# Second layer of a two-layer network: seven fp32 products replaced by three single passes over 12-bit parts

## The chip, the core and the metric

The kernel runs on one core of one Trainium2 chip. The metric is the device time of one execution in microseconds; shown for a kernel is the median of its runs. The profile is of one execution, whose own time is given beside its span. TensorE (PE) multiplies matrices, and each matmul has a weight load (PEld) of its own; VectorE (DVE) and ScalarE (ACT) do elementwise work, each in the order in which it was given; SyncE (SP) issues the DMAs, and waits in its own order too. Matmul results lie in eight banks of PSUM[...]; everything else lies in SBUF or in DRAM.

## What is computed

A gated linear attention with a recurrent state, and a network with a squared ReLU on its output:

```python
B, H, S, D = 4, 8, 768, 48
for t in range(S):
    state = alpha[:, :, t, :, None] * state + np.einsum('bhd,bhe->bhde', k[:, :, t], v[:, :, t])
    y[:, :, t] = np.einsum('bhd,bhde->bhe', q[:, :, t], state)
x = np.ascontiguousarray(y.transpose(0, 2, 1, 3)).reshape(B * S, H * D)   # 3072 x 384
h = np.maximum(x @ w_in, 0.0)                                           # w_in 384 x 2048
out = (h * h @ w_out).astype(np.float32)                                # w_out 2048 x 384
```

All inputs but the weights are fp32. The weights arrive as fp64 and are turned into fp32 by the kernel.

## The kernel before

The 3,072 tokens are 24 blocks of 128, block n being chunk n // 4 of batch n % 4. Four blocks are a group; there are six groups, g = 0 to 5 in the code (the change's "two to six" are g = 1 to 5). In group 0 the kernel loads and converts the weights and runs both layers plainly. From g = 1 on, a group is two stages of TensorE work, written out by hand, and the attention of the blocks of the next group is woven between their instructions.

**First layer, `layer_in`.** It follows the text `LAYER` word by word. `P` is a product (two matmuls of 128x256) into one of eight banks `b0` to `b7`: four from the pool `ps_att`, four from `ps_ffn`. A word such as `u3=u5+b7` is a DVE addition of 128x512, `u3=b1` a copy on ACT, `R` a ReLU and `Q` a square on ACT, `V` both at once on DVE. It is a scheme with fewer products than the plain one, over sums of parts of `x` (`sum_x`, 11 DVE operations, due at the end of the group before) and of `w_in`. Its results are the squared hidden values: `u0` to `u7` and `v0` to `v7`, 16 tiles of 256 hidden values by 256 tokens. `S` words add two of them for the second layer. `between` runs other steps ahead of a given word.

**Second layer, `ffn_product`.** A seven-product scheme for a two by two split matrix. For each product and each of four parts r there are four fp32 matmuls of 128x192, each of which shows as two records. 28 parts make a group. Between them DVE updates the operands (`s`, `a21`), and when a product ends, DVE and ACT add its result (`us`, `osb`); `store` writes the output. In g = 1, `sum_w_out` makes the sums of weight parts, 16 DVE operations of 384 columns.

**Weaving.** `weave(units, events)` issues the units in order; each has a cost, and an event is issued ahead of the first unit at which the running cost has reached its time. `attention(pairs, scale)` makes the events of a pair of blocks: by `PLAN`, `ln` (ACT) and `sp` (DVE splits the logarithm into two fp32r parts) come first, at 2.5 `cs` (TensorE sums the logarithms, `eb` and `ei` take exponentials on ACT), at 3.5 to 5 `mk` and `mq` (DVE scales keys and queries), at 6.5 `turn` (transposes), at 7 `kc` and `qc` (ACT copies), at 9.5 and 10.5 `ga` and `gb`: scores, state sums and the products `y` of the pair before, with DVE's masks and state updates. `gb` ends with `ev`, twelve ACT copies of the pair's `y` into `x`. `sum_x` follows at 11.5. The code issues in that order, and every engine keeps it. The pairs of a group before the change are

```python
pairs = [(0, n, True), (11.5, n + 2, True)]
if g == 1:
    pairs = [(0, n - 2, False), (6.8, n, True), (13.4, n + 2, True)]
```

The lines that matter: L674 products of the first layer, L616 all DVE additions made by `combine`, L685 `V`, L691 and L694 `Q` and `R`, L780 products of the second layer, L742 the plain second layer of group 0, L267 and L268 `cs` in fp32r, L283 `mk` and `mq`, L532 `turn`, L555 `ev`.

Of the kernel before, what the change touches and what calls it, by code (L numbers as in the profile page):

```python
# [25 lines left out]
def kernel(  # L26
# [64 lines left out]
    w_out = [consts.tile([128, NJ // NW, DM], FP32, name=f"w_out{i}") for i in range(NW)]  # L91
    HM, NR2 = DM // 2, NJ // 4
    tsum = [kept(f"t{i}_", NR2, [128, 2, HM]) for i in (1, 2, 4)]

    def flat(t):
        return t.rearrange("a x y -> a (x y)")

    lent = {("a", 2): flat(tsum[0][0]), ("a", 3): flat(tsum[0][1])}  # L100
    for x, n, i in (("q", 2, 6), ("q", 3, 7), ("k", 3, 5)):
        t = lent[x, n] = flat(w_out[i])[:, 0 : 64 * H].rearrange("a (h d) -> a h d", h=H)
        nc.gpsimd.memset(t[:, :, D:64], 0.0)
# [18 lines left out]
    def load_weights(i):  # L122
        dst = (w_in + w_out)[i]
        dt = moe_w_in.dtype
        raw = dst if dt == FP32 else raw_pool.tile(list(dst.shape), dt, tag="raw", name="raw")
        raws[i] = raw
        if i < NW:
            src = moe_w_in[:, i * DF // NW : (i + 1) * DF // NW]
            nc.sync.dma_start(out=raw, in_=src.rearrange("(k r) f -> r k f", r=128))
        else:  # L130
            i -= NW
            src = moe_w_out[i * DF // NW : (i + 1) * DF // NW, :]
            nc.sync.dma_start(out=raw, in_=src.rearrange("(j r) m -> r j m", r=128))
# [5 lines left out]

    def convert_first(i):  # L140
        if moe_w_in.dtype == FP32:
            return
        w = (w_in + w_out)[i].rearrange("a k f -> a (k f)")
        n = w.shape[1]
        words = raws.pop(i).rearrange("a k f -> a (k f)").bitcast(U32)
        words = words.rearrange("a (n h) -> a n h", h=2)
        lo, hi = words[:, :, 0], words[:, :, 1]
        power = cv_pool.tile([128, n], U32, tag="power", name="power")
        upper = cv_pool.tile([128, n], U32, tag="upper", name="upper")
        nc.vector.tensor_scalar(  # L150
            out=power, in0=hi, scalar1=20, scalar2=0x7FF,
            op0=ALU.logical_shift_right, op1=ALU.bitwise_and,
        )
        nc.vector.tensor_scalar(
            out=upper, in0=hi, scalar1=0xFFFFF, scalar2=None, op0=ALU.bitwise_and
        )
        half[i] = w, lo, hi, power, upper
# [72 lines left out]
    hid = [consts.tile([128, 2, GB * C], FP32, name=f"hid{i}") for i in range(NJ // 2)]  # L230
# [331 lines left out]
    def st(n):  # L562
# [34 lines left out]

# [7 lines left out]
        Pv4+w1x15 Qu2 v7=v5+b6 Pv3+w0x0 Ru7=-u7 u1=b4-u1 Pu7+w18x1 Qu7 v6=u1-b5 Pv1+w7x2 Su1  # L605
        Ru1=+b7 Pv4+w10x14 v0=v4-b3 Qu1 Pv6+w9x16 Rv4=+b1 V+v0 Pv5+w4x2 Qv4 v7=v7+b4 Pu2+w12x0
        v6=v6+b6 Rv7=-v7 v2=v2+b5 Pv0=w19x3 Qv7 V+v6 Rv2=+v2 Pv0+w6x1 Sv1 Qv2 Pu2+w7x2 v5=v5+b0
        Pu7=w19x3 Ru4=+b2 V+v5 Pu7+w6x1 Qu4 Pv4+w18x1 u5=u5+b7 V+u5 Rv1=+b4 Qv1 Su0 Sv0
    """
    FIRST = "u"  # L610

    acc, ws, sums = {}, {}, {}
# [10 lines left out]
    def w_slot(i):  # L623
# [4 lines left out]
        if r not in ws:  # L628
            ws[r] = raw_pool.tile([128, 3, 2, 256], FP32, tag="raw", name="ws")
            if r == 2:  # L630
                sums.update({3: ws[r][:, 2]})
# [12 lines left out]
    def sum_x(g):  # L644
        if not xs_ready:
            a = raw_pool.tile([128, 3, 2, HT], FP32, tag="raw", name="s012")
            sums.update({r: a[:, r] for r in range(3)})
            xs_ready.append(True)
# [3 lines left out]
    xs_ready = []  # L652

    def part(name):
        c, h = divmod(int(name[1]), 2)
        return hid[2 * c + "uv".index(name[0])][:, :, h * HT : (h + 1) * HT]

    def layer_in(g, between):
# [5 lines left out]
        for n, word in enumerate(LAYER.split()):  # L664
            if n in between:
                between[n]()
# [13 lines left out]
            elif word[0] == "S":  # L680
                r = 2 * int(word[2]) + "uv".index(word[1])
                combine(((sums[r], halves(r)[1], ALU.add, halves(NR2 + r)[1]),))
# [22 lines left out]
    def sum_w_out(i):  # L705
        i, r = divmod(i, NR2)
        t1, t2, t4 = (t[r] for t in tsum)
        b11, b12 = w_out[r][:, :, 0:HM], w_out[r][:, :, HM:DM]
        b21, b22 = w_out[NR2 + r][:, :, 0:HM], w_out[NR2 + r][:, :, HM:DM]
        o, x, z = ((t1, b12, b11), (t2, b22, t1), (b12, b22, b12), (t4, b21, t2))[i]  # L710
        combine(((o, x, ALU.subtract, z),))

    def halves(j):
        return hid[j][:, :, 0:HT], hid[j][:, :, HT : 2 * HT]

    turn_r = [0]

    def ffn_in(g, j, cols=slice(0, GB * C)):
# [11 lines left out]
        nc.scalar.activation(out=hid[j // 2][:, j % 2, cols], in_=r, func=AF.Square)  # L730
# [6 lines left out]
    def ffn_out(g, t, i):  # L737
# [3 lines left out]
        for j in range(per):  # L741
            nc.tensor.matmul(  # L742
                out=acc[t][:, 0:DM],
                lhsT=hid[i][:, j, t * C : (t + 1) * C],
# [13 lines left out]
    PRODUCTS = (("1", 0), ("5", 3), ("6", 1), ("7", 2), ("2", 0), ("4", 2), ("3", 3))  # L758

    R = [0, 2, 1, 3] if FIRST == "u" else [1, 3, 0, 2]  # L760
    PARTS = [(i, r) for rs in (R[:2], R[2:]) for i in range(2) for r in rs]
    PARTS += [(i, r) for i in range(2, len(PRODUCTS)) for r in R]

    def ffn_product(g, i, r):
        name, k = PRODUCTS[i]
        first = name in "1675"
        if r == R[0] and first:
            acc[k] = ps_ffn.tile([128, 2, HM], FP32, tag="f", name="o")
        (a11, a21), (a12, a22) = halves(r), halves(NR2 + r)
        s = sums[r]  # L770
        t1, t2, t4 = (t[r] for t in tsum)
        b11, t3 = w_out[r][:, :, 0:HM], w_out[r][:, :, HM:DM]
        b21, b22 = w_out[NR2 + r][:, :, 0:HM], w_out[NR2 + r][:, :, HM:DM]
        lhs, rhs = {
            "1": (a11, b11), "2": (a12, b21), "3": (s, b22), "4": (a22, t4),
            "5": (s, t1), "6": (s, t2), "7": (a21, t3),
        }[name]
        for j in range(2):
            for t in range(2):
                nc.tensor.matmul(  # L780
                    out=acc[k][:, t, :], lhsT=lhs[:, j, t * C : (t + 1) * C], rhs=rhs[:, j, :],
                    start=(first and r == R[0] and j + t == 0), stop=(r == R[-1] and j == 1),
                    skip_group_check=True,
                )
        if name == "5":
            combine(((s, s, ALU.subtract, a11),))
        elif name == "6":
            combine(((a21, a11, ALU.subtract, a21),))
        elif name == "7":
            combine(((s, a12, ALU.subtract, s),))  # L790
        if r != R[-1]:
            return
        if name == "1":
            for h in range(2):
                acc["out", h] = cv_pool.tile([128, 2, DM], FP32, tag="upper", name="osb")
            us = cv_pool.tile([128, 2, 2, HM], FP32, tag="power", name="us")
            acc["u1"], acc["u2"] = us[:, 0], us[:, 1]
            nc.scalar.activation(out=acc["u1"], in_=acc[k], func=AF.Copy)
        elif name == "5":
            pass  # L800
        elif name in "67":
            u, new = ("u1", "u2") if name == "6" else ("u2", "u3")
            if new == "u3":
                acc[new] = acc["out", 1][:, :, HM:DM]
            nc.vector.tensor_tensor(out=acc[new], in0=acc[k], in1=acc[u], op=ALU.add)
            if new == "u3":
                nc.vector.tensor_tensor(
                    out=acc[new], in0=acc[3], in1=acc[new], op=ALU.add
                )
        else:  # L810
            h, m, u = {"2": (0, 0, None), "4": (1, 0, "u2"), "3": (0, 1, "u2")}[name]
            o = acc["out", h][:, :, m * HM : (m + 1) * HM]
            if u:
                nc.vector.tensor_tensor(out=o, in0=acc[k], in1=acc[u], op=ALU.add)
            else:
                nc.scalar.activation(out=o, in_=acc[k], func=AF.Copy)
            if name in "43":
                for t in range(2):
                    store(g, 2 * h + t, acc["out", h][:, t, :])
            if name == "3":  # L820
                acc.clear()
# [96 lines left out]
    NG, NU = NBLK // GB, len(PRODUCTS) * NR2  # L918
# [9 lines left out]
    weave(units, sorted(events, key=lambda x: x[0]))  # L928
    for g in range(1, NG):

        between = {}
        if g == 1:
            between = {3 + 10 * i: lambda i=i: sum_w_out(i) for i in range(2 * NR2)}
        layer_in(g, between)
        events = []
        if g + 1 < NG:
            n = GB * (g + 1) + 2
            pairs = [(0, n, True), (11.5, n + 2, True)]
            if g == 1:
                pairs = [(0, n - 2, False), (6.8, n, True), (13.4, n + 2, True)]  # L940
            events = attention(pairs, 1) + [(pairs[-1][0] + 11.5, sum_x, (g + 1,))]
        if g == 1:
            late = [(0.5 + i, sum_w_out, (2 * NR2 + i,)) for i in range(2 * NR2)]
            events = sorted(events + late, key=lambda x: x[0])
        weave([(1, ffn_product, (g, *u)) for u in PARTS], events)
# [30 lines left out]
```

## Time and profile before

| | us |
|---|---|
| median of 3 runs (548.89 to 550.3) | 548.97 |
| the profiled execution | 549.13 |
| its span | 547.4 |
| first layer of a group, g = 1 to 5, TensorE | 34.53 |
| second layer of g = 5, with nothing woven in | 36.41 |
| from one first layer to the next, g = 2 to 3 | 84.87 |

The groups that cost DVE and ACT most, and the matmuls of the second layer (line, engine, operation, tiles written and read, shapes, count; busy us and mean ns of one; idle time just before them and what ended it):

```profile
L616 DVE TENSOR_TENSOR hid<-hid,h 128x512 f32<-128x512 f32 x130 | 88.4, 687 | 40.5 <-PE h L674 37.0
L780 PE MATMUL o<-w_out,hid 128*128 128x192 f32 x480 | 82.3, 327 | 0.0
L780 PEld LDWEIGHTS o<-w_out,hid 128*128 128x128 f32 x480 | 78.5, 190 | 0.6
...
L691 ACT ACTIVATE hid<-hid 128x512 f32<-128x512 f32 x55 | 34.7, 631 | 1.8
```

A matmul's 327 ns run from its issue to the end of its pipeline; the distance from start to start is what it takes of TensorE. DVE has long idle times ended by TensorE, and TensorE has none.

### The profile page before, as it was taken

What the parts mean: (1) busy time and instruction counts of PE and PEld (TensorE: products, weight loads), DVE (VectorE), ACT (ScalarE), POOL (GpSimd) and SP (SyncE); (2) the same over time, 40 slices, a digit from 0 to 9 for tenths busy, and PEclk for the clock granted to TensorE, in tenths of its full rate; (3) what the DMA queues carried; (4) which work ended last, traced back from release to release, by engine and by line L of the source; (5) the groups of instructions that cost most, each with busy time, mean ns of one, the idle gap of its engine ahead of it and who ended that gap; (6) DMA issues with size and microseconds to landing.
All of it is one profiled execution on the core that took longest, in us unless ns stands there. A gap on an engine that the chain in (4) does not pass through costs nothing.

```text
span 547.4 us, 12320 instructions
## 1 busy us (share of the span) xinstructions
PE 534.2 (98%) x5226; PEld 455.3 (83%) x5226; DVE 368.6 (67%) x656; ACT 235.8 (43%) x503; POOL 5.9 (1%) x26
## 2 busy tenths in 40 slices
PE   8889999999999999999999999999999999999996
PEld 5654456656889999989999988999988999988996
DVE  4888889993898873778583677673578651577530
ACT  4568874435264354246343236542326440336100
POOL 2010000000000000000000000000000000000000
PEclk9999999999999999999999999999999999999999
DMA  9979577201001664200343300252300000100001
GB/s 162 239 191 278 148 225 204 59 16 57 1 1 30 118 112 88 66 1 0 60 90 63 85 0 1 46 94 55 88 1 0 2 2 2 57 1 0 1 1 57
DMA packets 117085, 37.02 MB, mean 68 GB/s; under 512 B 108820, under 2 KB 111912, under 8 KB 117032
## 3 DMA queue, kind: packets, MB, share of 16 engines
q1 hardware_dynamic: 117032, 36.25, 29.5%
q8 instruction: 41, 0.67, 0.5%
q14 instruction: 12, 0.10, 0.1%
HBM read 31.49 MB, written 4.75 MB: 66 GB/s over the span
## 4 chain that ended last, share of the span: by engine, by line
PE 81%; DVE 10%; ACT 4%; issue 2%; DMA 2%; SPq 0%; POOL 0%; DVEq 0%; POOLq 0%
PE o L780 33%; PE h L674 32%; PE o L742 4%; PE y L397 4%; PE sckv L421 2%; PE T L532 2%; PE sckv L447 2%; ACT power L163 1%; DMA raw<-in_moe_w_in_dram 1%; DVE w_out L176 1%; DMA raw<-in_moe_w_out_dram 1%; DVE power L172 1%; DVE power L150 1%; DVE w_in L176 1%; DVE w_out L179 1%
## 5 line engine op out<-in xcount | busy, mean ns | idle before, releaser
L616 DVE TENSOR_TENSOR hid<-hid,h 128x512 f32<-128x512 f32 x130 | 88.4, 687 | 40.5 <-PE h L674 37.0
L780 PE MATMUL o<-w_out,hid 128*128 128x192 f32 x480 | 82.3, 327 | 0.0
L780 PEld LDWEIGHTS o<-w_out,hid 128*128 128x128 f32 x480 | 78.5, 190 | 0.6
L674 PE MATMUL h<-xs,w_in 128*128 128x256 f32 x320 | 74.8, 379 | 0.0
L555 ACT COPY x<-y 32x256 f32<-32x256 f32 (+2 forms) x132 | 46.3, 365 | 59.7 <-PE y L397 56.1
L674 PEld LDWEIGHTS h<-xs,w_in 128*128 128x128 f32 x320 | 60.7, 190 | 8.3
L674 PE MATMUL h<-x,ws 128*128 128x256 f32 x200 | 49.7, 379 | 0.0
L723 PE MATMUL h<-x,w_in 128*128 128x512 f32 (+1 forms) x108 | 43.5, 550 | 3.3 <-ACT x L555 1.8
L431 DVE COPY_PREDICATED am<-halves_mask,sckv 128x256 f32<-128x256 uint32 x40 | 15.5, 441 | 43.7 <-PE sckv L447 43.7
L698 ACT COPY hid<-h 128x512 f32<-128x512 f32 x20 | 11.7, 586 | 76.7 <-PE h L674 76.7
L780 PE MATMUL o<-t,s 128*128 128x192 f32 x240 | 43.2, 328 | 0.0
L742 PE MATMUL o<-w_out,hid 128*128 128x384 f32 x128 | 42.8, 490 | 0.0
L674 PEld LDWEIGHTS h<-x,ws 128*128 128x128 f32 x200 | 38.0, 190 | 5.2
L674 PE MATMUL h<-x,w_in 128*128 128x256 f32 x160 | 40.2, 379 | 0.0
L780 PEld LDWEIGHTS o<-t,s 128*128 128x128 f32 x240 | 39.5, 190 | 0.3
L723 PEld LDWEIGHTS h<-x,w_in 128*128 128x128 f32 x108 | 20.0, 190 | 23.4 <-issue 16.3
L742 PEld LDWEIGHTS o<-w_out,hid 128*128 128x128 f32 x128 | 23.9, 190 | 16.2 <-issue 0.5
L691 ACT ACTIVATE hid<-hid 128x512 f32<-128x512 f32 x55 | 34.7, 631 | 1.8
L674 PEld LDWEIGHTS h<-x,w_in 128*128 128x128 f32 x160 | 30.4, 190 | 4.1
L674 PE MATMUL h<-xs,ws 128*128 128x256 f32 x120 | 30.0, 379 | 0.0
L694 ACT ACTIVATE hid<-hid 128x512 f32<-128x512 f32 x35 | 22.0, 628 | 16.9 <-DVE hid L616 16.6
L780 PE MATMUL o<-t,hid 128*128 128x192 f32 x160 | 28.8, 331 | 0.0
(128 smaller groups left out, 764.8 us busy)
## 6 DMA issues: line engine op xcount, KB each, us to landing
raw<-in_moe_w_in_dram SPq DMA_DIRECT2D x8, 768.0 KB
raw<-in_moe_w_out_dram SPq DMA_DIRECT2D x8, 768.0 KB
v_in<-in_v_dram SPq DMA_DIRECT2D x24, 192.0 KB
out_dram<-osb SPq DMA_DIRECT2D x24, 192.0 KB
k_in<-in_k_dram SPq DMA_DIRECT2D x23, 192.0 KB
a_in<-in_alpha_dram SPq DMA_DIRECT2D x22, 192.0 KB
q_in<-in_q_dram SPq DMA_DIRECT2D x22, 192.0 KB
last<-row SPq DMA_DIRECT2D x40, 0.8 KB
```

Of the source, the lines that this page charges most:

```text
L176: nc.vector.scalar_tensor_tensor(out=w, in0=upper, scalar=2.0**-20, in1=w, op0=ALU.mult, op1=ALU.add)
L397: ins = nc.tensor.matmul(out=ys[e][64 * half : 64 * half + D + G * e, m % 2, p // 2, t], lhsT=lhsT, rhs=rhs, start=(half, e) not in seen, ...
L431: nc.vector.copy_predicated(out=am_h(n)[:, e, n % 2], data=ps[e][:, 0], mask=halves_mask.bitcast(U32).unsqueeze(1).to_broadcast([128, NP, ...
L555: copy(out=x[to : to + m, kk, t : t + 2], in_=blk[n]["y"][e][r : r + m, :, p // 2],)
L616: nc.vector.tensor_tensor(out=o, in0=x, in1=z, op=op)
L674: nc.tensor.matmul(out=banks[b][:, i, :], lhsT=w_slot(int(w))[:, "uv".index(p), i * 128 : (i + 1) * 128], rhs=x_slot(int(x)), start=(start ...
L691: nc.scalar.activation(out=t, in_=t, func=AF.Square)
L694: nc.scalar.activation(out=part(o), in_=operand(x), func=AF.Relu, scale=1.0 if sign == "+" else -1.0)
L698: nc.scalar.copy(out=part(word[0:2]), in_=operand(word[3:5]))
L723: nc.tensor.matmul(out=ps, lhsT=w[:, kk, c0 : c0 + 128], rhs=xT[g][:, kk, cols], start=(kk == 0), stop=(kk == KM - 1),)
L742: nc.tensor.matmul(out=acc[t][:, 0:DM], lhsT=hid[i][:, j, t * C : (t + 1) * C], rhs=w_out[i][:, j, :], start=(i == 0 and j == 0), stop=(i ...
L780: nc.tensor.matmul(out=acc[k][:, t, :], lhsT=lhs[:, j, t * C : (t + 1) * C], rhs=rhs[:, j, :], start=(first and r == R[0] and j + t == 0), ...
```

## The change

Each factor of the second layer is split into parts of at most 12 bits, [...]whose matmul shows as one record. A weight w is b + l with b the rounded part; a hidden value is a + l in the same way. The product is put together from three: a with b, l with l (the weights' l scaled by 2^12), and a difference of the hidden parts with a difference of the weights' parts. The first two are accumulated in one bank per block (stage one), scaled by 2^-12 into `osb` by ACT, and the third goes to the same bank (stage two) and is added to `osb` by DVE.

In g = 1 the first five pairs p of 256 hidden values in `ORDER` are done so, and the other three as plain fp32 matmuls; in g = 2 the weights of these three are split. The rounded weights stay in SBUF; `l` and `d` of the weights are written to DRAM once and read back in each later group through a ring of tiles. A unit of stage one is one pair p and one half h of the tokens: eight matmuls of 384 columns.

```diff
+    wt_pool = ctx.enter_context(tc.tile_pool(name="wt", bufs=14))
+    two_pool = ctx.enter_context(tc.tile_pool(name="two", bufs=19))
...
-        Pv4+w1x15 Qu2 v7=v5+b6 Pv3+w0x0 Ru7=-u7 u1=b4-u1 Pu7+w18x1 Qu7 v6=u1-b5 Pv1+w7x2 Su1
...
-        Pu7=w19x3 Ru4=+b2 V+v5 Pu7+w6x1 Qu4 Pv4+w18x1 u5=u5+b7 V+u5 Rv1=+b4 Qv1 Su0 Sv0
+        Pv4+w1x15 Qu2 v7=v5+b6 Pv3+w0x0 Ru7=-u7 u1=b4-u1 Pu7+w18x1 Qu7 v6=u1-b5 Pv1+w7x2 Ru1=+b7
...
+    def split_w(p):
+        b = w_out.pop(p)
+        parts_b[p] = wt("wb", FP32R)
+        nc.scalar.activation(out=parts_b[p], in_=b, func=AF.Copy, scale=NEAR)
+        parts_l[p] = wt("wl", FP32R)
+        nc.vector.tensor_tensor(
+            out=parts_l[p], in0=b, in1=parts_b[p].bitcast(FP32), op=ALU.subtract
+        )
+
+    def scale_w(p):
+        nc.scalar.activation(
+            out=parts_l[p], in_=parts_l[p].bitcast(FP32), func=AF.Copy, scale=1.0 / E
+        )
+        nc.sync.dma_start(out=dram_l[p], in_=flat(parts_l[p]))
...
+    def diff_w(p):
+        d = parts_d[p] = parts_l.pop(p)
+        nc.vector.tensor_tensor(
+            out=d, in0=parts_b[p].bitcast(FP32), in1=d.bitcast(FP32), op=ALU.subtract
+        )
+        nc.sync.dma_start(out=dram_d[p], in_=flat(d))
...
+    def split_h(n):
+        if n == 0 and not first_parts:
+            first_parts.append(raw_pool.tile([128, 3, 2, HT], FP32R, tag="raw", name="ha"))
+        a, l = first_parts[0][:, n % 3], two_k("hl", FP32R)
+        t = hid.pop(hs["units"][n])
+        nc.scalar.activation(out=a, in_=t, func=AF.Copy, scale=NEAR)
+        nc.vector.tensor_tensor(out=l, in0=t, in1=a.bitcast(FP32), op=ALU.subtract)
+        hs[n] = a, l
+
+    def diff_h(n):
+        a, l = hs[n]
+        d = hd[hs["units"][n]] = two_k("hd", FP32R)
+        nc.vector.scalar_tensor_tensor(
+            out=d, in0=a.bitcast(FP32), scalar=-E, in1=l.bitcast(FP32),
+            op0=ALU.mult, op1=ALU.add,
+        )
+
+    def of_piece(t, lhs, rhs, start=False, stop=False):
         for j in range(2):
+            nc.tensor.matmul(
+                out=acc[t][:, 0:DM], lhsT=lhs[:, j, t % 2 * C : (t % 2 + 1) * C],
+                rhs=rhs[:, j, :], start=start and j == 0, stop=stop or start,
+                skip_group_check=True,
+            )
+
+    def stage_one(g, n):
+        units = hs["units"]
+        p, h = units[n]
+        a, l = hs.pop(n)
+        for t in (2 * h, 2 * h + 1):
...
+            of_piece(t, a, parts_b[p], start=new)
+            of_piece(t, l, parts_l[p], stop=n >= len(units) - 2)
+        if n + 3 < len(units):
+            split_h(n + 3)
+            diff_h(n + 3)
...
+        if n % 2:
+            if g == 1:
+                diff_w(p)
+            else:
+                parts_l.pop(p)
...
+                to_stream and to_stream.pop(0)()
...
+    def layer_out(g):
+        order = UNITS[: len(UNITS) - 2 * len(PLAIN.get(g, ()))]
+        units = [(1, stage_one, (g, n)) for n in range(len(order))]
...
+        units += [(0.5, stage_two, (g, p, (h,))) for p, h in two_first]
+        units += [(1, stage_two, (g, p, (0, 1), p == ps[-1])) for p in ps[2:]]
+        return units
...
         if g == 1:
-            between = {3 + 10 * i: lambda i=i: sum_w_out(i) for i in range(2 * NR2)}
-        layer_in(g, between)
+            for i, p in enumerate(ORDER[:5]):
+                at(2 + 22 * i, split_w, p)
+                at(8 + 22 * i, scale_w, p)
+        else:
+            loads = ORDER[:RING]
+            if g == 2:
+                for i, p in enumerate(PLAIN[1]):
+                    at(2 + 12 * i, split_w, p)
+                    at(8 + 12 * i, scale_w, p)
+                    at(30 + 12 * i, diff_w, p)
...
+            for i, p in enumerate(loads):
+                at((70 if g == 2 else 20) + 5 * i, load_l, p)
+            for p in ORDER[RING:]:
+                to_stream.append(lambda p=p: load_l(p))
+            for p in ORDER:
+                to_stream.append(lambda p=p: load_d(p))
+        for n in range(3):
+            ready = max(done[hs["units"][n]] + 2, NWORDS - 24 + 8 * n)
+            at(ready, split_h, n)
+            at(ready + 4, diff_h, n)
         events = []
         if g + 1 < NG:
             n = GB * (g + 1) + 2
-            pairs = [(0, n, True), (11.5, n + 2, True)]
+            pairs = [(-2.5, n, True), (8.3, n + 2, True)]
             if g == 1:
-                pairs = [(0, n - 2, False), (6.8, n, True), (13.4, n + 2, True)]
+                pairs = [(-2.5, n - 2, False), (4.0, n, True), (10.5, n + 2, True)]
             events = attention(pairs, 1) + [(pairs[-1][0] + 11.5, sum_x, (g + 1,))]
...
+        for t, f, args in events:
+            if t < 0:
+                at(NWORDS - 20 + int(4 * t), f, *args)
```

`LAYER` has 101 words now. The tiles of `w_out` and of the hidden values come from the two new pools instead of constants, and tiles lent to the attention in group 0 come from the pool of hidden values.

## The prediction

> **What bounds the kernel now.** I read four views. First the page, for the shares of the engines:
>
> ```profile
> PE 534.2 (98%) x5226; PEld 455.3 (83%) x5226; DVE 368.6 (67%) x656; ACT 235.8 (43%) x503; POOL 5.9 (1%) x26
> ```
>
> Then the chain that ended last, in order of time (start, us, what). It shows whether that 98% is real, and the prices of both layers:
>
> ```profile
> 342.37 3.90 PE o L780 x24
> 346.98 5.20 PE o L780 x32
> 352.18 1.15 PE T L532 x32
> ...
> 472.28 34.53 PE h L674 x160
> 506.81 36.41 PE o L780 x224
> 543.25 0.56 DVE osb L814
> ```
>
> From 133 us on the chain is TensorE with hardly a hole. Each group is 34.53 us of first layer (160 records of 216 ns), 36.41 us of second layer (224 records of 162.5 ns) and, until g=4, some 14 us of attention for later blocks woven into the second layer. So TensorE work removed there is time won, and any wait of TensorE there is time lost. Two records stand for one fp32 matmul.
>
> Third, the timeline of TensorE around the only fp32r matmuls there are (the sums of logarithms), for the price of the new operation:
>
> ```profile
> 344.81 1.46 PE L780 MATMUL o<-t,s 128*128 128x192 f32 x8
> 345.98 0.47 PE L267 MATMUL cs<-hi,causal_r 128*128 128x384 f32 x1
> 346.29 0.34 PE L268 MATMUL cs<-lo,causal_r 128*128 128x384 f32 x1
> 346.46 0.34 PE L267 MATMUL cs<-hi,causal_r 128*128 128x384 f32 x1
> 346.64 0.34 PE L268 MATMUL cs<-lo,causal_r 128*128 128x384 f32 x1
> 346.82 0.81 PE L780 MATMUL o<-t,s 128*128 128x192 f32 x4
> ```
>
> The same tile shape as in the change (128x128 weights, 384 columns) starts every 0.17 to 0.18 us: 0.176, once, where fp32 takes two records.
>
> Fourth, the timeline of DVE and ACT, for paces and waits, and the busy time by stretch at the end of the first layer of g=2 (us, PE, PEld, DVE, ACT, POOL):
>
> ```profile
> 247.64 0.68 DVE L616 TENSOR_TENSOR s<-hid,hid 128x512 f32<-128x512 f32 x1
> 248.25 0.68 DVE L616 TENSOR_TENSOR hid<-hid,h 128x512 f32<-128x512 f32 x1
> 248.96 0.69 DVE L685 SCALAR_TENSOR_TENSOR hid<-hid 128x512 f32<-128x512 f32 x1
> ...
> 264.04 0.55 DVE L283 TENSOR_TENSOR k_in<-k_in,inv 128x384 f32<-128x384 f32 x1
> 264.51 0.55 DVE L283 TENSOR_TENSOR q_in<-q_in,b 128x384 f32<-128x384 f32 x1
> ```
>
> ```profile
> 123.79 4.35 ACT L555 COPY x<-y 32x256 f32<-32x256 f32 x12 [9.64 <-PE y L397]
> 128.18 0.43 DVE L616 TENSOR_TENSOR xs<-xs,x 128x256 f32<-128x256 f32 x1 [4.96 <-ACT x L555]
> ```
>
> ```profile
> 248.00:253.00 5.00, 5.00 (x25) 4.40 (x24) 4.50 (x8) 4.36 (x8) 0.00 (x0) 1.00 0.00 0
> 253.00:257.50 4.50, 4.50 (x23) 3.96 (x22) 2.56 (x5) 1.73 (x3) 0.00 (x0) 1.00 0.00 0
> ```
>
> A 128x512 DVE operation costs 0.60 us if it doesn't read the one before (247.64 to 248.25), 0.72 if it does (248.25 to 248.96); one of 384 columns 0.47. DVE and ACT are nearly full just before the first layer ends. Twelve copies and the sums after them are a chain of 4.4 us plus.
>
> [...]
>
> **TensorE, part by part.** In g=2 to 5 the second layer goes from 224 records x 0.1625 = 36.4 us to 3 x 64 fp32r matmuls x 0.176 = 33.8: -2.6 each, -10.4. In g=1 five of eight pairs are in parts (120 x 0.176 = 21.1) and three stay plain fp32 without the seven-product scheme (24 matmuls of 384 columns, 48 records x 0.3225 from L742 = 15.5): 36.6, +0.2. Sum -10.2. Bounds on the pace: 0.1625 (the fp32 records) gives -22.2; 0.178 (longest fp32r) -8.4.
>
> **DVE and ACT.** Removed in a group: 4 S sums and 12 updates of the operands (0.69 each, busy) and a few adds of 0.55. Added: 16 subtractions and 16 scalar_tensor_tensor, 1.32 us a unit, and 16 ACT copies of 0.6. A unit (8 matmuls) lasts 1.41 us on TensorE, so DVE keeps up, with 7% to spare and attention on top. The ring of three `ha` means that splitting unit n+3 starts only when TensorE has left unit n: 2.8 us for ACT 0.6, DVE 0.7 and three signals: about 1.1 us spare. No wait from this alone.
>
> End of the first layer, g>=2. By the order of instructions DVE now gets, from word 69, the two log splits (pace 0.39 + 0.52, twice: 1.8 us) and three unit splits (six operations, 3.6) among the ten it had; four S go. From 247.64, where Su1 stood: 1.8, then v0, V, split, v7, v6, diff, v2, split, V, diff, v5, split, V, diff, u5, V at 0.6 (0.72 behind a dependence) ends at 259.4. TensorE ends the layer at 257.1 in any case, as the banks it needs are read earlier; so DVE is 2.3 us late.
>
> Stage one from there (zero = 257.1): cs to 0.7, units 0 to 3 until 6.35, then the transposes of `turn`, formerly 1.5 units later. They need mq1, which stands on DVE behind the splits of units 3, 4, 5: split 3 starts 3.1 (its ACT copy is behind b and inv), then 0.72, 0.6, 0.47 (mk0), 0.72, 0.6, 0.47, 0.47, 0.72, 0.6: mq1 runs 8.4 to 9.0. TensorE would be at the last eight transposes at 7.2: wait 1.7 us, x3 (g=2,3,4) = 5.1. Bounds 0 to 3 each.
>
> Copies of `ev` in gb before unit 8: ACT is blocked 4.4 us from 0.75 us after gb begins; the copy of unit 11 ends at 5.8, its subtraction at 6.6; TensorE (1.85 of gb, three units) arrives at 6.1: 0.5, x3 = 1.5. Bounds 0 to 1.3 each.
>
> g=1. Five weight splits replace 16 half-size sums: at words 68 and 90 they add 2 x 0.87 on DVE and about 1 us of waiting for ACT just where it is full, so it is some 5 us late. The second half of unit 1 needs a bank that u5 must leave: 1.9 us. mq1 comes later still, behind a `diff_w`: 2.8. And the weave counts a plain unit as 1 though it takes 5.2 us, and the group has 18 units: the last ga (20) and gb (21), and sum_x (22), fall behind the last unit. The order shows scores, y, scores, then the first layer at once. Nothing covers them: twelve copies 4.4, signals 0.3, four sums 1.5, the wait from ga to gb 0.5, less 1.1 of TensorE work: 5.6 us (4.5 to 7). Before, four units, 5.2 us of TensorE, stood behind gb there. Sum for g=1: 10.3.
>
> g=2, first layer: three weight splits and three diffs, 5.2 us of DVE by word 54, where, by the timeline, u2, u3 and u5 end under 0.5 us before TensorE reuses the bank that they read: I take 1.5 (0 to 4).
>
> At nothing: DRAM traffic, 6.3 MB a group, because each part is asked for 7 us or more before its use (cover gone: see the rivals); the last loads d6 and d7 have five units, 7 us. SP blocks in program order only. At the boundaries of g=2 to 4 gb has five units behind it, 8.9 us of TensorE against 7.0 for copies and four sums. The tail (add, store) stays. Group 0 has the same instructions in the same order.
>
> **Sum.** -10.2 + 10.3 + 1.5 + 5.1 + 1.5 = +8.2. The profiled execution took 549.13 us (span 547.4 and 1.7 to 1.8 around it; the median shown is 548.97): 557.
>
> **Rivals.** (1) The fp32r stream runs at 0.1625, if the 0.176 belongs to the short bursts: -22.2; but a unit is then 1.30 us, DVE's 1.32 binds and waits grow by about 2: 549.1 - 22.2 + 20.4 = 547. Against it: eight bursts, all 174 to 178 ns, and fp32 right behind is at 162. (2) The other side: DVE isn't late at the end of the first layer, as DVE had 1.9 us and ACT 2.8 us idle in the last window shown and could take the splits there. If its lag is under 0.7 us, the waits on turn and on the bank vanish and only the g=1 boundary and ev stay: 549.1 - 10.2 + 7.1 = 546. Against it: ten operations and six more don't fit into 8.6 us. (3) Parts from DRAM come late, behind attention loads of 1,024 packets of 192 B or a store that SP waits for. Two waits of 2 us in each of g=2 to 5: 557 + 16 = 573. For it: the DMA share reaches 0.65 in one window; against: 3 KB packets and wide margins.
>
> **Numbers.** Forecast 0.60, rival 1 0.12, rival 2 0.19, rival 3 0.09. The 0.3% that a measurement can tell from no change is 1.6 us. Rival 2 and most of rival 1 are faster, with a little from the low end of the forecast: 0.27; within 0.3%: 0.08; slower 0.65. The forecast's own range is 550 to 565; with the rivals of the other sign the range is 541 to 566. Half of the DVE waits would give about 552.
>
> **What would show it.** Second layer of g=5 near 33.8 us with starts 0.176 apart (TensorE); T behind DVE q_in in g=2 to 4 by 1 to 2 us; an idle stretch of 5 us ahead of the first layer of g=2, ended by DVE xs; unit 1 of g=1 behind DVE hid. If T waits under 0.5 us, rival 2; starts of 0.163, rival 1; waits on wl or wd, rival 3.

## The result and the profile after

The changed kernel takes 570.38 us (median of 4 runs, 567.51 to 571.65) against 548.93 (4 runs, 548.59 to 550.3): a ratio of 1.0379, interval 1.0333 to 1.0424. The profiled execution took 571.2 us, its span is 569.4. The forecast was 557, so it was right that the kernel gets slower, and 13 us short of the median.

First the page of the changed kernel: busy time, share and instructions of each engine, and the granted clock of TensorE in 40 equal slices (9 is full).

```profile
PE 537.5 (94%) x5042; PEld 446.5 (78%) x5042; DVE 415.0 (73%) x719; ACT 292.0 (51%) x603; POOL 5.9 (1%) x26
...
PEclk9999999999998999799999999989999989999999
```

TensorE's share fell from 98% to 94%, and in four slices the clock isn't full. Then the chain that ended last (start, us, what):

```profile
237.13 24.52 PE h L681 x100
...
328.36 34.53 PE h L681 x160
...
372.29 5.89 PE o L827 x24
379.27 1.43 PE y L412 x88
...
531.90 32.97 PE o L827 x190
```

The last line is the second layer of g=5 with nothing woven in. Its records are those of fp32r, the type of the new parts, one for a matmul (192 in all); they start 173 to 174 ns apart, and from first record to end the stage takes 33.7 us where it took 36.6. The first layer is 34.53 as before. So the gain is there; from the start of one first layer to the next (g=5: to TensorE's end) the rest shows:

| us | g=1 | g=2 | g=3 | g=4 | g=5 |
|---|---|---|---|---|---|
| before | 90.00 | 84.88 | 84.50 | 79.94 | 71.10 |
| after | 103.54 | 91.07 | 88.05 | 80.96 | 68.00 |

Which waits are new, by the list of waits (engine and line that waited, for what: us, times, longest):

```profile
PEld T L547 <- DVE q_in L298: 8.6, 8, 1.5
PE T L547 <- DVE q_in L298: 7.4, 7, 1.4
PEld h L681 <- ACT wb L779: 5.2, 1, 5.2
PE h L681 <- DVE xs L628: 5.1, 1, 5.1
```

The lower two are one idle stretch, that ahead of g=2; there the name of ACT's `wb` is misleading, as DVE's `xs` came last. In g=3, the timelines of DVE and TensorE show the wait of the transposes and what follows it:

```profile
369.35 0.55 DVE L298 TENSOR_TENSOR k_in<-k_in,inv 128x384 f32<-128x384 f32 x1
369.82 0.68 DVE L814 TENSOR_TENSOR hl<-hid,ha 128x512 fp32r<-128x512 f32 x1
370.61 0.69 DVE L820 SCALAR_TENSOR_TENSOR hd<-ha,hl 128x512 fp32r<-128x512 f32 x1
371.22 0.55 DVE L298 TENSOR_TENSOR q_in<-q_in,b 128x384 f32<-128x384 f32 x1
```

```profile
369.96 0.46 PE L547 MATMUL T<-ident,k_in 64*128 64x64 f32 x8
371.82 0.46 PE L547 MATMUL T<-ident,q_in 64*128 64x64 f32 x8 [1.40 <-DVE q_in L298]
372.22 1.01 PE L827 MATMUL o<-wb,ha 128*128 128x384 f32 x2
373.02 0.84 PE L827 MATMUL o<-wl,hl 128*128 128x384 f32 x2
...
375.93 0.51 PE L827 MATMUL o<-wb,ha 128*128 128x384 f32 x2
```

The scaled `q` stands on DVE behind a unit's split and difference, and TensorE loses 1.67 us. DVE and ACT keep the order of the code: in this trace the 175 DVE and 130 ACT operations of the five passes through `LAYER` stand in the order of its words. Then the same pair of matmuls takes 0.84 us until 375.6, and 0.51 after it: the records show a granted clock of one half for 3.41 us from 372.2. Such stretches begin at 174.2, 198.1 (it lies across two slices and does not show in the row above), 235.6 (two in a row), 372.2 and 460.9, each behind idle time of TensorE, and lengthen TensorE's work by 1.57, 1.57, 2.31, 1.78 and 1.57 us (distances from record to record less those usual for their kind): 8.8 us. The kernel before had none until TensorE's last matmul. The other new wait is in front of the second block's sum of logarithms in the second pair; ACT and DVE in g=3:

```profile
383.52 4.35 ACT L570 COPY x<-y 32x256 f32<-32x256 f32 x12
387.90 1.67 ACT L813 ACTIVATE ha<-hid 128x512 fp32r<-128x512 f32 x3
```

```profile
388.56 0.69 DVE L814 TENSOR_TENSOR hl<-hid,ha 128x512 fp32r<-128x512 f32 x1 [1.67 <-ACT ha L813]
389.36 0.69 DVE L820 SCALAR_TENSOR_TENSOR hd<-ha,hl 128x512 fp32r<-128x512 f32 x1
389.97 0.35 DVE L270 CAST hi<-a_in 128x384 fp32r<-128x384 f32 x1
390.35 0.56 DVE L271 TENSOR_TENSOR lo<-a_in,hi 128x384 fp32r<-128x384 f32 x1
```

Unit 11's copy `ha` stands behind the twelve copies of `x`, its split waits for that copy on DVE, and `hi` and `lo` stand behind the split: TensorE loses 2.48 us at `cs` here and 2.05 in g=2, counted in the same way.

### The profile page after: what moved, and what is told of

It is laid out like the page before. It is cut to its first block, busy times and chain, and to the rows that moved or that the text cites. A ratio compares the mean times of both kernels' runs of the same rounds, so it can differ in the third digit from the quotient of the medians.

```text
span 569.4 us, 12387 instructions
## 1 busy us (share of the span) xinstructions
PE 537.5 (94%) x5042; PEld 446.5 (78%) x5042; DVE 415.0 (73%) x719; ACT 292.0 (51%) x603; POOL 5.9 (1%) x26
## 4 chain that ended last, share of the span: by engine, by line
PE 65%; DVE 20%; ACT 10%; issue 4%; DMA 1%; DVEq 0%; SPq 0%; POOL 0%; ACTq 0%; POOLq 0%
PE o L827 26%; PE h L681 26%; PE o L737 4%; PE y L412 3%; DVE hl L814 2%; DVE hd L820 2%; ACT x L570 2%; PE T L547 1%; ACT power L178 1%; DVE hid L628 1%; PE sckv L436 1%; ACT hid L698 1%; DVE q_in L298 1%; DVE w_out L191 1%; DVE k_in L298 1%
## 5 line engine op out<-in xcount | busy, mean ns | idle before, releaser
L827 PE MATMUL o<-wb,ha 128*128 128x384 f32 x296 | 80.1, 352 | 2.3 <-ACT hid L698 2.0
L827 PE MATMUL o<-wl,hl 128*128 128x384 f32 x296 | 77.9, 345 | 0.1
L681 PEld LDWEIGHTS h<-xs,w_in 128*128 128x128 f32 x320 | 62.5, 196 | 14.2 <-ACT wb L779 5.2
L813 ACT ACTIVATE ha<-hid 128x512 fp32r<-128x512 f32 x74 | 46.0, 634 | 49.3 <-PE o L827 36.8
L814 DVE TENSOR_TENSOR hl<-hid,ha 128x512 fp32r<-128x512 f32 x74 | 50.9, 688 | 20.3 <-ACT ha L813 19.4
L827 PEld LDWEIGHTS o<-wb,ha 128*128 128x128 f32 x296 | 54.9, 196 | 4.1 <-ACT hid L698 2.3
L827 PEld LDWEIGHTS o<-wl,hl 128*128 128x128 f32 x296 | 55.5, 195 | 0.5 <-DVE hl L814 0.4
L820 DVE SCALAR_TENSOR_TENSOR hd<-ha,hl 128x512 fp32r<-128x512 f32 x74 | 51.1, 690 | 4.1 <-PE o L827 0.6
L827 PE MATMUL o<-wd,hd 128*128 128x384 f32 x256 | 46.7, 337 | 0.0
L827 PEld LDWEIGHTS o<-wd,hd 128*128 128x128 f32 x256 | 44.2, 188 | 0.4
L737 PEld LDWEIGHTS o<-w_out,hid 128*128 128x128 f32 x128 | 23.9, 190 | 16.2 <-issue 0.5
```

Source lines behind the costliest of these rows:

```text
L681: nc.tensor.matmul(out=banks[b][:, i, :], lhsT=w_slot(int(w))[:, "uv".index(p), i * 128 : (i + 1) * 128], rhs=x_slot(int(x)), start=(start ...
L737: nc.tensor.matmul(out=acc[t][:, 0:DM], lhsT=hid0[per * i + j][:, t * C : (t + 1) * C], rhs=w_out[i][:, j, :], start=(i == 0 and j == 0), ...
L813: nc.scalar.activation(out=a, in_=t, func=AF.Copy, scale=NEAR)
L814: nc.vector.tensor_tensor(out=l, in0=t, in1=a.bitcast(FP32), op=ALU.subtract)
L820: nc.vector.scalar_tensor_tensor(out=d, in0=a.bitcast(FP32), scalar=-E, in1=l.bitcast(FP32), op0=ALU.mult, op1=ALU.add,)
L827: nc.tensor.matmul(out=acc[t][:, 0:DM], lhsT=lhs[:, j, t % 2 * C : (t % 2 + 1) * C], rhs=rhs[:, j, :], start=start and j == 0, stop=stop o ...
```

## The experiments

Theory A: the loss is waits that come from the places of instructions, and on top of each the clock that idle time costs. Rivals: B, the clock drops are no cost of their own; C, DVE and ACT are full, so a wait taken away comes back; D, the traffic to DRAM. All edits are of the changed kernel. A quoted text is what was expected before the run; waits and times by group are those of the run's one profiled execution, the time measured is the median of all its executions.

### Is the clock a cost of its own?

Products that nobody reads (`keep_busy`: `ident` by `causal`) in TensorE's idle time, first in four places:

```diff
             for i, x in enumerate("kq"):
+                if m in (11, 19, 23) and x == "q":
+                    keep_busy(ps[0][:, 1].rearrange("a p t -> a (p t)")[:, 0:128], 6)
...
+                    if g == 2 and n == 0:
+                        keep_busy(banks[b][:, 0, 0:128], 22)
```

> Fp32 products whose result nobody reads (ident by causal, 128 columns) stand where TensorE waits: six ahead of the last eight transposes of three turns (the second turn of g=1, the first of g=3 and of g=4), 22 ahead of the first product of g=2. The waits themselves are left as they are. Theory A (the clock follows TensorE's own idle stretches, and the halved clock is a cost of its own): no stretch of half clock at 198, 236, 372 and 461 us, one left at 174; time 570.4 - (1.57 + 2.31 + 1.78 + 1.57) = 563, and the wait for q_in or xs ends at the same distance from what stands before it. Rival B (the clock drops are an outside disturbance of the chip, or cost nothing because the waits that follow shrink by as much): 570 or more, with as many stretches of half clock as after.

Measured: 573.36, a miss for A, and as long as B had said; but two things spoil the reading. All five stretches of half clock were gone, and four others had come, at 35.2, 182.0, 284.4 and 393.6. And the 22 products could start only at 235.0, when ACT's copies of `x` had left their bank, and so held up g=2 by 3 us. Only g=4 is a clean reading: 79.45 for 80.96. The second try fills more places, and less in each:

```diff
+    FILL = {9: 5, 11: 4, 15: 5, 17: 2, 19: 5, 21: 2, 23: 5}
...
+                if x == "q" and m in FILL:
+                    keep_busy(ps[0][:, 1].rearrange("a p t -> a (p t)")[:, 0:128], FILL[m])
...
+        if n in (17, 21):
+            keep_busy(out[:, 0:128], 6)
...
+        if g == 2:
+            keep_busy(ps_ffn.tile([128, GB * C], FP32, tag="f", name="idle")[:, 0:128], 21)
```

> As the first experiment, but with products whose result nobody reads in all the longer waits, fewer than fit (0.235 us each): five, four, five, five and five ahead of the last transposes of the first turns of g=1, the second of g=1, the first of g=2, 3, 4; two in the second turns of g=2 and 3; six ahead of the second sum of logarithms of the second pair; 21 (4.9 us for a wait of 5.6) ahead of the first product of g=2, in a bank that is free early. Theory A (idle TensorE drops the clock, in windows that no instruction chooses, and the drop costs time of its own): the waits end where they ended, at most two stretches of half clock are left (at 173 and in group 0), and the time is 570.4 - 7.2 = 563 (562 to 565.5). Rival B (the clock costs nothing of its own): 570 or more.

Measured: 566.65 (566.29 to 566.84). TensorE's timeline of this run at the same turn of g=3, and its clock by slices:

```profile
367.07 0.46 PE L559 MATMUL T<-ident,k_in 64*128 64x64 f32 x8
367.46 1.38 PE L545 MATMUL T<-causal,ident 128*128 128x128 f32 x10
368.94 0.46 PE L559 MATMUL T<-ident,q_in 64*128 64x64 f32 x8
369.33 0.62 PE L841 MATMUL o<-wb,ha 128*128 128x384 f32 x2
369.79 0.51 PE L841 MATMUL o<-wl,hl 128*128 128x384 f32 x2
```

```profile
PEclk9999999999998999999999999999999999999999
```

The wait is as long as before (1.87 us from the transposes of `k` to those of `q`, for 1.86), the matmuls behind it are at 0.51 from the second pair on, and one stretch is left. TensorE does more work and the kernel is 3.7 us faster: B is refuted. It is half of the 7.2 expected. In the profile, g=2 gave 2.6 and g=4 1.6, g=1 and g=3 nothing: four products in g=1 stood where there was no wait (0.9), and TensorE, earlier now, waited more at `y`, state sums and scores (1.1 in g=1; 2.0 for 0.4 in g=3), at products that wait for no other engine (more on these under the traffic). So the 8.8 us are what the slow stretches add to the matmuls in them; how much of it the kernel would gain without them stays open.

The cleanest price needs no filling. In g=4 three kernels (the changed one and two variants below that leave g=4 alone) had a stretch of half clock behind the wait at the turn: 80.96, 80.99 and 80.97. Two other variants that leave g=4 alone had the same wait and no such stretch: 79.37 and 79.41. With the wait filled it was 79.38. Half clock costs 1.6 us there.

When does it drop? Of the changed kernel and its variants, 15 profiles have stretches of half clock after the first 20 us. In each of them all of these begin on one grid of 3.413 us; in the changed kernel's, the five places lie 7, 11, 40 and 26 steps apart. Sorted by the share of a window of this grid in which TensorE's records show it busy, all 27 windows under 52% were followed by half clock, 16 of 34 between 52 and 60%, and 7 of over 2,200 above (six of them the first window of a double stretch, itself at half clock). In the changed kernel's profile the 1.40 us of idle ahead of the transposes at 371.82 lie inside one window (368.74 to 372.15, 59% busy), and half clock follows; the 1.41 us ahead of those at 284.13 are cut in two by a boundary at 283.41 (windows 64 and 79% busy), and none follows. Windows in which the records leave 1.3 to 1.9 us idle were enough. This fits the scatter: the changed kernel's times lie 4 us apart, with a mean clock of 0.988 in the fastest execution and 0.979 in the slowest, those of the run just shown 0.6 us apart, at 0.996 to 0.999.

### Are the waits of place?

The first pair of g=2 to 4 later:

```diff
-            pairs = [(-2.5, n, True), (8.3, n + 2, True)]
+            pairs = [(-1.0, n, True), (8.3, n + 2, True)]
```

> The first pair of attention in g=2, 3 and 4 stands 1.5 units later (-1.0 for -2.5), so that the transposes have unit 4 and 5 ahead of them. Theory A: the three waits of the transposes for q_in (1.67 each) fall to under 0.3, and with them the half clock at 372 and 461 (1.78 and 1.57): 570.4 - 4.2 to 5.0 - 3.4 = 562 to 563. Rival C (DVE and ACT are simply too full in these stages, and any place gives the same wait): the wait moves to the sums of logarithms, to units 5 to 8 or to gb, and the time stays at 569 to 571.

Measured: 561.65, just under Theory A's 562 to 563. In g=2 to 4 (87.24, 85.19, 78.71) the waits for `q_in` are under 0.3, and no half clock follows the turns. But `gb` comes later too: in g=2 and 3 `cs` waited some 1.1 us for the copies of `x` to leave its bank.

The end of g=1:

```diff
+        for p in ps[2:]:
+            if p in PLAIN.get(g, ()):
+                units += [(1.85, stage_two, (g, p, (h,), p == ps[-1])) for h in range(2)]
+            else:
+                units.append((1, stage_two, (g, p, (0, 1), p == ps[-1])))
...
-                pairs = [(-2.5, n - 2, False), (4.0, n, True), (10.5, n + 2, True)]
+                pairs = [(-2.5, n - 2, False), (4.0, n, True), (9.1, n + 2, True)]
```

> In g=1 the plain units are halved and counted at 1.85 each, as they last on TensorE, and the last pair stands at 9.1, so that its gb and the sums of x have two of them and more (5 to 8 us of TensorE) behind them. Theory A: the 5.63 us of idle ahead of g=2 fall to 0 to 1, and the half clock of 235.6 to 242.4 goes with it (2.31): 570.4 - 4.6 to 5.6 - 2.3 = 562.5 to 563.5. Rival (the copies and sums wait for something else than their place): the idle stretch stays over 3 us and the time over 567.

Measured: 567.13, a miss. The idle stretch ahead of g=2 was gone, but g=1 took 103.13. The third pair's `hi` now stood on DVE ahead of the second pair's last `q_in` and itself waited 2.9 for a DMA, so that the second turn waited 4.0; and TensorE waited 1.5 for ACT's `osb`. With only `ga`, `gb` and the sums earlier (`t` is 10.25 for that pair alone):

```diff
+                    if t == 10.25 and f in ("ga", "gb"):
+                        w -= 1.2
```

> In g=1 the plain units are halved and counted at 1.85 each; the last pair keeps its place (10.25 for 10.5), only its ga, gb and the sums of x come 1.2 earlier, so that three halves (7.8 us of TensorE) stand behind gb. Theory A: nothing else in g=1 moves, the 5.63 us of idle ahead of g=2 and the half clock there go: 570.4 - 5.6 - 2.3 = 562.5 (561.5 to 565, if another idle stretch meets the window instead). Rival: as in the experiment with the whole pair moved, other waits of g=1 take most of it back: over 567.

Measured: 562.28, a hit; the idle stretch was gone and g=1 took 97.97.

The second pair's logarithms ahead of `gb`:

```diff
-                    w = t + at * scale
+                    w = t + at * scale - (0.4 if f == "sp1" and t == 8.3 else 0)
```

> In g=2 and 3 the split of the logarithms of the second block of the second pair stands on DVE ahead of gb and of unit 11, not behind them. Theory A: the waits of cs ahead of unit 9 to 11 (2.05 in g=2, 2.48 in g=3) go; unit 11 itself, whose copy stands on ACT behind the twelve copies of x, then waits 0.5 as predicted: 570.4 - 3.5 = 567 (566.5 to 568). Rival (the copies of x hold ACT long enough that unit 11 takes over the wait in full): 569.5 to 570.5.

Measured: 566.77, a hit; the waits of `cs` were gone, g=2 and 3 fell by 1.75 and 2.2. Part came back at the next turn (1.35 and 1.41 for `q_in`).

The weight splits of g=1:

```diff
-                at(2 + 22 * i, split_w, p)
-                at(8 + 22 * i, scale_w, p)
+                at(2 + 12 * i, split_w, p)
+                at(8 + 12 * i, scale_w, p)
```

> The five weight splits of g=1 stand at words 2 + 12i and 8 + 12i of the first layer for 2 + 22i and 8 + 22i, so that none is left on DVE and ACT from word 57 on. Theory A: DVE and ACT are no longer late at the end of the first layer of g=1, unit 1 waits under 0.5 instead of 2.29 + 0.56, and the half clock at 174 goes: 570.4 - 2.3 - 1.6 = 566 to 566.5. Rival C (the splits of logarithms and units alone make DVE late there, as in g=2 to 4): unit 1 still waits over 1.5 and the time is over 568.5.

Measured: 567.56, between the two. Unit 1 no longer waited 2.29 + 0.56, the half clock at 174 was gone, and g=1 fell by 3.8; but g=2 rose by 2.9 in the profiled run, though nothing was changed there: its old wait at the turn fell into a window of the clock, and half clock ran from 280.1 to 286.9.

### Does the traffic matter?

```diff
+        nc.sync.dma_start(out=spare[p], in_=dram_l[p])
...
+        nc.sync.dma_start(out=spare[NW + p], in_=dram_d[p])
```

> Behind each load of a part in g=2 to 5 stands a second transfer of the same part from DRAM to a spare place in DRAM, so that these 64 loads cause over twice the traffic. Theory A (the parts arrive long before use): no wait of TensorE for wl or wd, 570.4 within 1.5. Rival D (parts from DRAM and the queue are near their limit): waits for wl or wd of 2 us and more in each of g=2 to 5, 578 or more.

Measured: 576.59, 6.2 slower than the changed kernel. Neither theory had it right: nobody waits for `wl` or `wd`, and the traffic costs time all the same. In the profile g=2 alone lost 7.6, with three more stretches of half clock and this wait in the middle of the state sums:

```profile
322.25 0.68 PE L462 MATMUL sckv<-v_in,k_in 64*64 64x64 f32 x29
326.00 0.33 PE L462 MATMUL sckv<-v_in,k_in 64*64 64x64 f32 x3 [3.06 <-issue]
```

It lies between the 29th and the 30th of 32 like products, where no record waits for a semaphore; that is what "issue" says. What the trace has there is a DMA of 16 KB of the kind "instruction", from 323.72 on, 2.28 us before the matmul. This is no exception: of the 51 waits of over 0.4 us that the 17 profiles have inside the runs of small products (`y`, scores, state sums) from g=1 on, 50 end 2.2 to 3.0 us after such a DMA began. That TensorE waits there for its own instructions is a guess from these times; no experiment tests it. These waits add up to 1.5 us after the change and to 6.5 at twice the traffic, but also to 4.6 in the first run with products that nobody reads, so that their growth with the traffic is likely and not shown.

### Does it add up, and is there a floor?

All edits together (in g=1 also -1.5 for -2.5 and 4.5 for 4.0), then the first pair of g=2 to 4 at -2.0:

> All four edits of place together: first pair of g=2 to 4 at -1.0, last pair of g=1 with its ga, gb and sums ahead of three halves of plain units, logarithms of the second pair first, weight splits of g=1 early; and in g=1 the first pair at -1.5 for -2.5, the second at 4.5 for 4.0. Theory A (the loss of the change is waits of place and the clock that they cost, each removable alone): the gains measured one by one add up, 8.7 + 8.1 + 2.8 to 4.4, and 1 to 3 of the 3.6 for the logarithms, as part of that wait is already gone: 570.4 - 22 = 548.5 (545 to 551), level with the kernel before. Rival C (DVE and ACT are full, so a wait removed comes back elsewhere): over 554.

> As the run with all edits, with the first pair of g=2 to 4 at -2.0, between the two: its transposes stand one unit later than after the change, its gb one unit earlier than at -1.0, so that the second pair's sums of logarithms have three units, not one, between them and the copies of x that free their bank. Theory A: the wait for q_in leaves 0.3 (1.67 - 1.41), the waits of cs for ACT's copies of x (0.8 + 0.4 in g=2 and 3) go: 1 to 3 below the run at -1.0, 546.5 (544 to 550). Rival C: at or above the run at -1.0.

Measured: 554.6 and 553.77. The gains did not add up: 15.8 of the 22 us came. The profiled execution at -2.0 was the fastest of six (550.52, the others from 553.5 on). In it g=2 to 5 took 83.94, 83.21, 78.06 and 68.00: all below the kernel before, by 7.2 us in all. g=1 took 98.3, and there a removed wait had come back, as C says: unit 1 no longer waits, so the transposes came sooner and waited 1.3 and 2.6 for `mk` and `mq`, with 6.8 us of half clock. DVE there, in the run at -2.0:

```profile
177.52 0.68 DVE L814 TENSOR_TENSOR hl<-hid,ha 128x512 fp32r<-128x512 f32 x1
178.31 0.69 DVE L820 SCALAR_TENSOR_TENSOR hd<-ha,hl 128x512 fp32r<-128x512 f32 x1
178.92 0.95 DVE L793 TENSOR_TENSOR wl<-wb,wl 128x768 fp32r<-128x768 f32 x1
179.78 0.55 DVE L298 TENSOR_TENSOR q_in<-q_in,b 128x384 f32<-128x384 f32 x1
```

DVE has no gap, and a weight difference stands ahead of the last factor. So the factors of g=1 were put together, and then the differences later:

```diff
+                    if t in (-1.5, 4.5) and f[:2] in ("mk", "mq"):
+                        w = t + 3.5
...
-                diff_w(p)
+                for q in ([], [], [0], [1], [2, 3, 4])[n // 2]:
+                    diff_w(units[2 * q][0])
```

> As the run with all edits and the first pair of g=2 to 4 at -2.0; and in g=1 the four products of k and q with their factors (mk, mq) of the first and second pair stand on DVE one behind the other, at 3.5 units after the pair's start, with no unit split and no diff of weights between them. Theory A: of the turn waits left in g=1 (1.3 + 2.6 at 177 and 180, 0.85 + 1.05 at 197) under 1 is left in all, and the half clock of 179.7 to 186.5 (2.8) goes: 553.8 - 4.8 - 2 = 547 (545 to 549.5), at or under the kernel before. Rival C (DVE is full there: the unit splits pushed back by 1.9 us hold up units 5 to 7 instead): 551 or more.

> The same, and in g=1 the diffs of the weights (0.9 us each on DVE) stand two pairs of units later, behind the first turn. Theory A: where the four products together removed the waits, nothing is left to gain, 547 within 1; where some wait is left ahead of the transposes of g=1, it shrinks by up to 1.8. Rival C: the three diffs together at the end of stage one hold up the factors of the second and third pair, 1 to 3 above the run without this edit.

Measured: 549.95 with the first edit (ratio 1.0013 to the kernel before, interval 1.0003 to 1.0023), 550.45 with both; the first lies between the two theories, and the second edit gained nothing. With the first, the first turn no longer waits, but `cs` of the second pair waits 3.0 for `hi` and `lo`, and the second turn 1.8 for a `k` that arrives late. Two runs tried that place alone, without the later differences, the first with an earlier load of `k` too:

```diff
+                    if t == 4.5 and f[:2] in ("ln", "sp"):
+                        w = t - (2.0 if f[:2] == "ln" else 1.6)
...
+                            if t == -1.5:
+                                out.append((w, load, (n0 + 3, "k")))
```

> As the run with the factors together; and in g=1 the k of block 11 is asked for at the first turn, ahead of the q, not at the first ga (DVE waited 1.63 for its arrival), and the logarithms of the second pair are taken and split ahead of the split of unit 6 (cs waited 0.76 + 0.36 + 1.56 + 0.35 for them). Theory A (also the rest of g=1 is place): these 4.8 us fall to under 1.5, with the half clock at 195 (1.6): 549.95 - 4.5 = 545.5 (544 to 548), under the kernel before. Rival C (DVE and ACT have no room left in g=1, as the splits of units 6 and 7 come 1.8 us later): 549 to 551, with the wait at units 6 or 7.

> As the run with the factors together, with the logarithms of the second pair of g=1 taken and split ahead of the split of unit 6, and the load of k left where it was. Theory A: the wait of cs (3.0) goes, the wait for k of block 11 stays: 549.95 - 3 = 547. Rival C (DVE has no room there): unit 6 waits 1.5 to 2 instead, 548.5 to 550.5.

In the first, the `k` of block 11 takes the buffer of block 8's before that block's state sums, which so read the `k` of block 11: this kernel leaves out a needed `k`, and only its time is used. Measured: 551.99 and 551.24. The wait of `cs` had become one of 1.57 and 1.58 of unit 6 for its split, as C says. That isn't all: in the second the wait for the `k` of block 11, a DMA and not DVE's work, grew from 1.8 to 3.9, and half clock ran for 6.8 us in place of 3.4. Last, both places together, with the transfers of the differences off SP (in the profile of the changed kernel SP issued nothing from 173.45 to 179.06, when the first difference was done):

```diff
-        nc.sync.dma_start(out=dram_d[p], in_=flat(d))
+        nc.gpsimd.dma_start(out=dram_d[p], in_=flat(d))
```

> The same, and room is made: the diffs of the weights of g=1 stand two pairs of units later (1.9 us of DVE less ahead of the splits of units 5 to 8), and their transfers to DRAM are issued by GpSimd, so that SP does not stand ahead of the loads of k until a diff is done. Theory A (the rest of g=1 is place and queues): neither cs nor unit 6 waits over 0.5, the wait for k shrinks: 546 (544.5 to 547.5), under the kernel before. Rival C (g=1 is full for DVE): 548.5 or more.

Measured: 547.47 (546.69 to 548.16), ratio 0.9968 to the kernel before, interval 0.9956 to 0.9979: inside Theory A's range, and 0.3% faster than the kernel before (all of its seven executions lie below the eleven of that kernel beside them, 548.72 to 550.53). Its page:

```profile
PE 526.2 (96%) x5042; PEld 437.6 (80%) x5042; DVE 413.5 (76%) x719; ACT 293.5 (54%) x603; POOL 10.4 (2%) x34
...
PEclk9999999999999999999999999999999999999999
```

g=1 took 95.03, still 5.0 more than before: unit 6 waits 1.0 for its split, more than Theory A had, the second turn no longer for `k` but 1.4 for banks that DVE still reads, and a `y` product 1.9 in the way told under the traffic. DVE does nearly what it did after the change (413.5 us for 415.0); only the order is another. Which of the later differences and the freed SP counted was not tried apart.

## Why the prediction was wrong

- **The step that failed** is the sum: it counts each wait of TensorE at its own length, with TensorE's pace the same behind it. In fact idle time also halved the clock, for 3.41 us at a time: 8.8 us of slower matmuls, which no term or rival held. It is the largest part of the 14.2 between 557 and the profiled 571.2. That it costs time is shown by g=4 with and without such a stretch (1.6 us) and by filling the idle time, which gave back 3.7 in all, with the filling's own cost in it.
- TensorE: right in kind and size. Taken 0.176 us, -2.6 a group; found 0.173 to 0.174 and -3.1 (71.10 to 68.00), some 2 us more gain in all. Rival 1 (0.1625) is refuted. That all eight bursts showed 174 to 178 ns was read too widely: in the two at 281.9 and 366.8 starts lie 0.3 to 0.5 us apart.
- The turn in g=2 to 4: 1.7 each predicted, 1.67 each measured, at the instruction named. Rival 2 (DVE isn't late) falls.
- The boundary ahead of g=2: 5.6 predicted, 5.63 measured (5.30 in one stretch, 0.33 between `ga` and `gb`), mechanism as told and shown by the run that took it away. The 0.3 for signals was an estimate; in the profile 0.06 us lie between the last `y` and ACT's copies at 231.17, and 0.15 between DVE's `xs` and TensorE at 237.13.
- The rest of g=1: unit 1, 1.9 predicted, 2.29 + 0.56 measured (it ends with DVE's `u5` as told, but its first half waits already, for the bank that ACT's last `R` reads); first turn 2.8, measured 0.46 + 0.28 + 1.60; the second turn's 1.43 + 0.33 was not predicted.
- `ev`: "0.5, x3" was mis-sized. The copies hold up unit 11 as predicted, but I did not ask what stands behind its split on DVE: `hi` and `lo`, so that `cs`, ahead of unit 11, waits first. 2.05 + 2.48 + 0.39 (g=4, unit 11 itself), 3.4 more than the 1.5 taken.
- The first layer of g=2: 1.5 predicted for the weight splits, nothing found; its 2.31 are the clock.
- DRAM at nothing: right for `wl` and `wd`, which nobody waits for, even at twice the traffic; rival 3's waits did not occur, and that its 573 comes near to the time is luck. That the traffic costs nothing isn't shown: twice the traffic cost 6.2 us, and how is open.
- Group 0 at nothing: right. It took 0.8 us more in the profile, but with its instructions the same it took 132.6 to 133.8 us in the runs above, 132.8 before.

The misses add to 8.8 + 3.4 + 1.8 + 0.9 - 0.5 - 1.5 - 2 = 10.9; the rest is 0.8 of scatter in group 0 and waits of 0.3 to 1.1 at turns and inside `y` and scores.

## What to carry to other kernels

Where TensorE sets the time, don't price a new wait at its length alone: in these profiles half clock followed every window of 3.413 us that was under 52% busy and 16 of 34 between 52 and 60%, one stretch of it cost 1.6 us in g=4, and filling the waits gave back 3.7 of the 7.2 us expected. Read the clock row first when a sum of waits falls short. Removing one wait proves little on an engine without gaps: follow the instructions queued behind it, and count a gain only when the next one is seen to hold. A unit's cost in a weave must be its true duration, or what is due late falls off the end.

## What the runs showed that was not expected

The clock's grid keeps its phase through an execution (the four stretches of the first filling run, 35.2 to 393.6, lie 43, 30 and 32 steps of 3.413 us apart) and can have another one in the next (its first boundary after the first instruction falls at 0.1 us in the changed kernel's profile and at 1.1 in that run), which is the likely reason why kernels with waits of 1.5 to 2 us scatter: in the 22 runs with the factors together, 549.95 in the median, the mean clock went from 0.997 (548.9 to 550.1 us) to 0.990 (553.1). With four idle stretches filled, five drops were gone and four others had come. The fp32r matmuls start 173 to 174 ns apart in a stream of 190 for 384 columns, while the fp32 records of 192 columns, two for a matmul, start 162.5 ns apart. And what the profile calls "issue" inside runs of small products comes with a DMA of instructions in 50 of 51 cases, at 2.2 to 3.0 us from its start.
